# Another table of places: more sums by adding transfers, evictions on VectorE, loads on GpSimd's queue

## The chip, the cores and the metric

The kernel runs on one core of one Trainium2 chip. The metric is the device time of one execution in microseconds, and the figure used is the median over several runs. The core's engines are named as the profile names them: PE (TensorE, matrix products), PEld (its weight loads), DVE (VectorE), ACT (ScalarE), POOL (GpSimd) and SP (SyncE, which here only issues transfers). Each engine carries out its own instructions strictly in order; where one needs the result of another engine or of a transfer, it waits on a semaphore, and everything behind it on that engine waits too.

## What is computed

There are 2048 rows of 640 columns. The first half of the reference is a long convolution, done there by FFT, between a layer norm and a gate; the second half is a SwiGLU feed-forward network with a layer norm ahead of it. Both have a residual.

```python
def _A_ref(q, k, v, shift_k, ssm_k, ssm_D):        # B, S, D = 1, 2048, 640
    k_pad = jnp.pad(k, ((0, 0), (ks - 1, 0), (0, 0)))
    for t in range(ks):                            # ks = 4
        k_shift = k_shift + k_pad[:, t:t + S, :] * shift_k[:, ks - 1 - t][None, None, :]
    kv = k_shift * v
    ...
    y_f = kv_f * kf_f[None, :, :, :]
    y = irfft2(y_f, ...)[:, 0, :S, :]              # causal convolution of kv with ssm_k
    y = y + kv * ssm_D[None, None, :]
    return q * y

def _B_ref(x, w_gate, w_up, w_down):               # 640 -> 1728 -> 640
    g = _silu(x @ w_gate)
    u = x @ w_up
    return (g * u) @ w_down

x = A_q
h = x + _A_ref(_layernorm(x, axis=-1), A_k, A_v, A_shift_k, A_ssm_k, A_ssm_D)
h2 = h + _B_ref(_layernorm(h, axis=-1), B_w_gate, B_w_up, B_w_down)
return h2
```

## The kernel before

**Blocks.** The rows are cut into four blocks of 512 (0 to 3). A block lies in SBUF as 128 partitions with four rows each, a tile of 128x2560 elements in bf16 (640 KB). The convolution is done block by block in a transformed space of length 1024: the filter's block j gives the spectrum G_j, the input's block j the spectrum X_j, and block j of the output needs the products of all pairs X_i, G_(j-i).

**Stages of one block.** Block j runs through these steps; the lines are those of the profile.
- Loads of the filter (L289), k (L477 for block 0, transposing transfers for the others), v (L296) and q (L301). The filter is copied by rows on ACT and transposed by four transfers (L404); block 0's is transposed on PE (L411, evicted at L413).
- kv: four shifted products of k with a diagonal matrix on PE (L490, L492), evicted and multiplied by v.
- Spectra: matrix products with the table WF on PE (L329), each evicted from PSUM in the function `taken`, by ACT (L319) or by DVE (L322); then differences and sums of the halves on DVE (L361, L379, L386, L390, L393). L393 is the sum that may be a transfer.
- Products: for each pair, L539 or L542 on DVE multiplies two spectra (128x2560 for L542), and the sums of such products are L545. Two closing lines, L581 and L582, put real and imaginary parts together. Block 1 has two pairs, block 2 three, block 3 four.
- Inverse: L662, L663, L674 and L677 on DVE, matrix products with the table WI on PE (L698), a scaling on ACT (L707), and L709 on DVE, which multiplies by the normalised q, adds q and gives h.
- The second layer norm: sums of squares on ACT (L606), three small DVE steps (L644, L646, L648) with one on POOL between them (L610); the normalised row is written by ACT (L722) or DVE (L724), and transposed.
- Feed-forward of the block before, spread between the stages of the present one: gate and up products on PE (L769); Silu on ACT (L783); then either a copy of the up half on ACT (L785) with a product of two SBUF tiles on DVE (L787), or a product straight from PSUM on DVE (L786); L811 closes the last, half-wide chunk; the products with w_down on PE (L833, L845), the eviction on ACT (L850) and an adding store on GpSimd's queue (L852), or L862 and a plain store (L866) for the last block. Ahead of a block's adding stores, h itself is stored (L754).

**What sets the order.** The program first builds 923 operations in a `Plan`, each with its reads and writes, and then emits them in the order of the table `ORDER` (L48 to L90). The compiler leaves that order alone, so the table alone decides what stands behind what on each engine. An entry `i` emits operation i as built. An entry that is negative emits operation `~i` (that is -i-1) in its *other* form, which three kinds of operations and two single ones have:
- `evict` and `taken`, the row at L722 and the up half at L785 are built for ACT and have a form for DVE (for L785 that form is L786, and L787 falls away);
- `added` (sums L393 and L545 and the like) is built for DVE and has a form in which GpSimd's queue carries a transfer from one SBUF tile into another that adds on arrival (L243);
- `load` (L250) is built for SP's queue and has a form on GpSimd's.

```python
def added(ns, fn, to, what, reads, write, n=1):
    plan.add("dve", ns, fn, reads, [write], ("add", 2 * P * R * D * n,
        lambda: nc.gpsimd.dma_start(out=to(), in_=what(), accum_op=ALU.add, max_dma_last_dim=4 * D)))

def load(nbytes, fn, w, r=()):
    return plan.add("sp", nbytes, lambda: fn(nc.sync), r, w, ("pq", nbytes, lambda: fn(nc.gpsimd)))
```

**Places and queues.** Tiles of 640 KB come from an arena of 22 units; besides there are four PSUM slots of two banks, five row tiles and three tiles for the gate. A unit goes to the next user in the order of the table, and the user waits until the former one is done. SP's queue and GpSimd's have eight semaphores each (DMAHW0 to 7, DMASW0 to 7), used in turn: a transfer that would take a semaphore whose last transfer is still under way waits for it, and so do those behind it in the same queue. POOL also does a few small steps of its own (L610, L624, L634 to L636).

## Time and profile before

| | before |
|---|---|
| runs, us | 251.36, 251.21, 253.07 |
| median, us | 251.36 |
| span of the profiled execution, us | 251.4 |
| PE busy, us (share) | 237.3 (94%) |
| DVE busy | 197.7 (79%) |
| ACT busy | 173.9 (69%) |
| POOL busy | 54.0 (21%) |
| adding transfers between SBUF tiles (L243) | 11 |
| moved by SP's queue / GpSimd's, MB | 21.38 / 11.96 |

A busy share is an average over the whole span. Which engine sets the time is seen stage by stage: the stretch in which an engine has no idle time, and who waits for it there. The chain of waits that ended last goes back from the last instruction to what released it at each step, and so shows at which engine the path changes hands. A tile's buffer number is left out in the views (arena, ps, sg), so a line and an operation say what stands there.

### The profile page before, as it was taken

The page shows a single profiled execution, that of the slowest core. Times are in us where ns is not written, and L with a number is a line of the kernel's source. Part 1 is how long each engine was busy: PE and PEld are TensorE (multiplying, and loading weights), DVE is VectorE, ACT ScalarE, POOL GpSimd, SP SyncE. Part 2 cuts the span into 40 slices and gives each one's busy share as a digit, 9 for nine tenths or more (in the row PEclk, how much of TensorE's full clock was granted, in tenths as well). Part 3 has the DMA queues.
Part 4 walks back from the last instruction along what each step waited for, and adds up shares of the span by engine and source line. Part 5 has one row for each costly group of instructions (what it writes and reads, how often), then busy time and mean ns, then how long its engine had stood idle before and what let it go on. Part 6 is the DMA issues. An engine that isn't in the chain of part 4 may idle for free.

```text
span 251.4 us, 5138 instructions
## 1 busy us (share of the span) xinstructions
PE 237.3 (94%) x2113; PEld 153.0 (61%) x2125; DVE 197.7 (79%) x249; ACT 173.9 (69%) x300; POOL 54.0 (21%) x54
## 2 busy tenths in 40 slices
PE   3869997999999999999999999999999999999994
PEld 3447675788777677444465676454456785465662
DVE  2379999999999999999999989999999542131222
ACT  2449998999999976975988789983542865325100
POOL 0002003231540313220270404263612110000030
PEclk9999999999999999999999999999999999999999
DMA  5995699774998654685345468889592200000052
GB/s 156 376 212 163 127 324 352 231 197 92 165 246 292 202 81 81 105 154 133 79 66 146 86 99 194 148 146 163 98 224 29 26 0 3 0 0 3 0 78 78
DMA packets 37283, 33.66 MB, mean 134 GB/s; under 512 B 22470, under 2 KB 32076, under 8 KB 37260
## 3 DMA queue, kind: packets, MB, share of 16 engines
q1 hardware_dynamic: 31884, 21.38, 32.1%
q0 software_dynamic: 5376, 11.96, 25.9%
q8 instruction: 16, 0.26, 0.4%
q14 instruction: 7, 0.06, 0.1%
HBM read 16.29 MB, written 4.59 MB: 83 GB/s over the span
## 4 chain that ended last, share of the span: by engine, by line
PE 56%; ACT 17%; DMA 10%; DVE 9%; issue 4%; SPq 3%; DVEq 0%; ACTq 0%; POOLq 0%
PE ps L769 24%; PE ps L845 22%; ACT arena L319 7%; DMA arena<-in_A_ssm_k_dram 7%; PE ps L698 5%; DMA arena<-arena 3%; ACT sg L785 2%; PE ps L490 2%; SPq L404 2%; ACT junk L606 1%; PE ps L329 1%; PE ps L833 1%; DVE arena L674 1%; DVE arena L663 1%; DVE arena L662 1%
## 5 line engine op out<-in xcount | busy, mean ns | idle before, releaser
L769 PE MATMUL ps<-arena,wgu 128*128 128x512 bf16 (+1 forms) x668 | 116.7, 328 | 1.4 <-ACT sg L809 0.5
L769 PEld LDWEIGHTS <-wgu 128*128 128x128 bf16 x680 | 66.2, 98 | 45.3 <-issue 1.4
L845 PE MATMUL ps<-wd,tT 128*128 128x320 bf16 x416 | 59.1, 299 | 0.0
L845 PEld LDWEIGHTS <-tT 128*128 128x128 bf16 x416 | 39.8, 98 | 17.2 <-issue 1.8
L542 DVE TENSOR_TENSOR arena<-arena 128x2560 bf16<-128x2560 bf16 x30 | 44.1, 1484 | 0.2
L783 ACT ACTIVATE sg<-ps 128x1024 bf16<-128x1024 f32 (+1 forms) x28 | 26.9, 968 | 20.3 <-PE ps L769 19.7
L329 PE MATMUL ps<-arena,WF 128*128 128x320 bf16 x176 | 29.8, 299 | 1.2 <-ACT arena L319 0.9
L785 ACT CAST sg<-ps 128x1024 bf16<-128x1024 f32 (+1 forms) x23 | 23.0, 998 | 6.9 <-PE ps L769 3.1
L319 ACT CAST arena<-ps 128x320 bf16<-128x320 f32 (+1 forms) x48 | 25.2, 583 | 1.9 <-DVE arena L545 1.1
L610 POOL TENSOR_TENSOR sm<-sm,neghalf 128x4 f32<-128x4 f32 (+1 forms) x10 | 16.6, 1659 | 43.4 <-DVE sm L646 43.1
L787 DVE TENSOR_TENSOR tT<-sg,sg 128x1024 bf16<-128x1024 bf16 (+1 forms) x23 | 15.5, 673 | 11.5 <-ACT sg L785 11.5
L243 POOL DMA_DIRECT2D arena<-arena x11 | 13.3, 1211 | 47.4 <-DVE arena L542 11.2
L329 PEld LDWEIGHTS <-WF 128*128 128x128 bf16 x176 | 17.1, 98 | 10.0 <-issue 2.3
L606 ACT ACTIVATE junk<-arena 128x640 bf16<-128x640 bf16 x28 | 20.8, 744 | 1.3 <-DVE arena L709 1.3
L545 DVE TENSOR_TENSOR arena<-arena 128x2560 bf16<-128x2560 bf16 x14 | 20.7, 1487 | 0.2
L319 ACT ACTIVATE arena<-ps 128x640 bf16<-128x640 f32 (+1 forms) x32 | 20.2, 655 | 0.3
L698 PE MATMUL ps<-arena,WI 128*128 128x320 bf16 x96 | 15.7, 299 | 0.9 <-issue 0.6
L850 ACT ACTIVATE row<-ps,sm 128x640 bf16<-128x640 f32 x12 | 9.5, 791 | 8.2 <-PE ps L845 8.0
L709 DVE SCALAR_TENSOR_TENSOR arena<-arena,sm,ps 128x640 bf16<-128x640 bf16 x16 | 13.6, 876 | 1.8 <-ACT ps L707 1.8
L852 POOL DMA_DIRECT2D out_dram<-row x12 | 11.7, 1153 | 14.1 <-ACT row L850 14.1
L707 ACT ACTIVATE ps<-ps,sm 128x640 f32<-128x640 f32 x16 | 12.1, 770 | 3.7 <-PE ps L698 3.5
L698 PEld LDWEIGHTS <-WI 128*128 128x128 bf16 x96 | 9.0, 97 | 5.6 <-issue 1.3
(91 smaller groups left out, 240.8 us busy)
## 6 DMA issues: line engine op xcount, KB each, us to landing
arena<-arena POOLq DMA_DIRECT2D x11, 640.0 KB, 6.1
arena<-in_A_q_dram SPq DMA_DIRECT2D x4, 640.0 KB, 5.1
out_dram<-row POOLq DMA_DIRECT2D x13, 160.0 KB, 4.2
arena<-in_A_ssm_k_dram SPq DMA_DIRECT2D x3, 640.0 KB, 9.4
arena<-in_A_v_dram SPq DMA_DIRECT2D x3, 640.0 KB, 6.3
wd<-in_B_w_down_dram SPq DMA_DIRECT2D x2, 800.0 KB, 7.3
out_dram<-arena POOLq DMA_DIRECT2D x2, 640.0 KB, 5.8
wgu<-in_B_w_gate_dram SPq DMA_DIRECT2D x1, 800.0 KB, 6.5
```

The source lines that it names most:

```text
L319: (lambda: nc.scalar.activation(dst(), src(), ACT.Copy, scale=2.0)) if twice else (lambda: nc.scalar.copy(dst(), src())),
L329: nc.tensor.matmul(ap(ps)[:, h, 0:NH], w, ap(src)[:, r, h * NH:(h + 1) * NH], start=(first and i == 0), stop=(last and i == len(rs) - 1), ...
L542: dve(1402, lambda: v.tensor_mul(to(), X.part(xs), H.part(hs)), [X.at(xs), H.at(hs)], [at])
L545: added(1402 * n - 69 * (n - 1), lambda: v.tensor_add(to(), to(), b()), to, b, [what], at, n)
L606: act(725, lambda r=r: nc.scalar.activation(waste(), ap(x)[:, r, :], ACT.Square, scale=D ** -0.5, accum_out=sm(s, MSQ, (r,))), [(x, r)], [ ...
L610: nc.gpsimd.tensor_tensor(sm(s, RSTD, rs), sm(s, VAR, rs), ap(neghalf)[:, 0:len(rs)], op=ALU.pow)
L698: nc.tensor.matmul(ap(ps)[:, w, 0:NH], m, src[:, w * NH:(w + 1) * NH], start=(i == 0), stop=(i == len(terms) - 1))
L769: nc.tensor.matmul(split(ap(ps), n)[:, i, :], w(k), ap(hT)[:, k, lo:lo + n], start=(k == 0), stop=(k == KT - 1))
L783: act(905 if wide_ else 490, lambda: nc.scalar.activation(of(sg), of(*gate), ACT.Silu), [(gate[0], gate[1] + i) for i in range(m)] + (psu ...
L785: op = plan.add("act", 905 if wide_ else 490, lambda: nc.scalar.copy(of(co), of(*up)), psu + [sg], [co] + tt, ("dve", 1135 if wide_ else 6 ...
L787: op.rest = dve(602 if wide_ else 336, lambda: nc.vector.tensor_mul(to(), of(sg), of(co)), [sg, co], tt)
L845: nc.tensor.matmul(ap(ps[hf])[:, hf, 0:NH], ap(tT)[:, c * BLK + at:c * BLK + at + P], ap(wd)[:, c, hf * NH:(hf + 1) * NH], start=False, st ...
```

## The change

Only the table `ORDER` differs; no operation is added or taken away, and PE carries out the same products. It places most of the 923 operations in another order, and takes other forms:
- Adding transfers instead of DVE sums: 22 instead of 11. Block 1 has six (two before), block 2 seven (two), block 3 nine (seven).
- Twenty evictions more are DVE's than before (26 go from ACT to DVE, six go back). To DVE go two transposes of block 0 (L413), six half-wide L319s of block 0's spectra and six whole ones of later blocks (then L322), six rows of L722 (then L724), and six up halves of L785 (then L786 in the place of L785 and L787).
- GpSimd's queue carries 18 loads and plain stores instead of five. Sixteen are new on it: the taps, block 0's filter, the skip weights, block 0's q and one half of WI at the start; four loads of FFN weights; q of blocks 1 to 3; block 2's filter; and three stores of output rows of the last block. Three go back to SP's: block 0's store of h, and block 3's filter and v.

The first rows of the table, of 43 that all change:

```diff
-    0, 1, 2, 3, 16, 18, -20, 5, 4, 8, 17, 186, 9, 20, 22, 7, 10, 11, -22, 24, -26, 23, 26, 75, 76, 13, 15, 12, 6,
-    77, 78, 79, 193, 80, 81, 82, 34, 35, 14, 38, -40, 36, -38, 92, 32, 27, 93, 96, 97, 40, -42, 88, 89, 30, 94,
...
+    -9, 16, 5, 0, 3, 9, 10, 18, 19, -16, 7, 11, 20, 17, 24, 25, -13, -22, 1, 22, -24, 26, 75, 2, 76, 77, 6, 78, 79,
+    80, 83, 81, 186, 82, 36, 34, 40, 13, 37, -36, -42, 109, 42, 14, 88, 96, 38, -40, 110, 111, -113, 32, 89, 90,
...
```

SP's queue at the start, before: k's two halves (L477), the taps (L889), block 0's filter (L289), v (L296), the tables WF (L903) and WI (L909), the skip weights (L904), block 1's filter (the second L289) and q (L301).

```order
L477 DMA arena_86<-in_A_k_dram 128x1280
L889 DMA arena_86<-in_A_shift_k_dram 5x512
L477 DMA arena_86<-in_A_k_dram 128x1280
L289 DMA arena_86<-in_A_ssm_k_dram 128x5x512
L296 DMA arena_86<-in_A_v_dram 128x2560
L903 DMA WF_88<-const_wf 128x1024
L904 DMA arena_86<-in_A_ssm_D_dram 1x640
L289 DMA arena_86<-in_A_ssm_k_dram 128x5x512
L903 DMA WF_88<-const_wf 128x1024 [waits DMAHW0_49]
L301 DMA arena_86<-in_A_q_dram 128x2560 [waits DMAHW1_49]
L909 DMA WI_89<-const_wi 128x1024 [waits DMAHW2_49]
L909 DMA WI_89<-const_wi 128x1024 [waits DMAHW3_49]
```

The same queue after, down to the first load that waits for a semaphore. L404 is a transposing transfer of block 1's k, L737 a load of FFN weights.

```order
L477 DMA arena_86<-in_A_k_dram 128x1280 x2
L296 DMA arena_86<-in_A_v_dram 128x2560
L289 DMA arena_86<-in_A_ssm_k_dram 128x5x512
L903 DMA WF_88<-const_wf 128x1024 x2
L404 DMA_TRANSPOSE kT_93<-in_A_k_dram 128x5x128 [waits Activation_49]
L909 DMA WI_89<-const_wi 128x1024
L737 DMA wgu_95<-in_B_w_up_dram 128x5x512 [waits DMAHW0_49]
```

And GpSimd's queue after, from its first transfer to the load of block 2's filter (the second L289); before, this engine had no transfer ahead of its 13th row, block 0's store of h. L872, L875, L624 and L610 are POOL's own steps.

```order
L889 DMA arena_86<-in_A_shift_k_dram 5x512
L872 ISA
L872 AFFINE_SELECT ident_87<-ident_87 128x128 [waits DVE_49]
L904 DMA arena_86<-in_A_ssm_D_dram 1x16x40
L289 DMA arena_86<-in_A_ssm_k_dram 128x5x512
L301 DMA arena_86<-in_A_q_dram 128x2560
L909 DMA WI_89<-const_wi 128x1024
L875 MEMSET neghalf_99 128x4
L624 TENSOR_SCALAR sm0_76<-sm0_76 128x4 [waits DVE_49]
L610 TENSOR_TENSOR sm0_76<-sm0_76,neghalf_99 128x4 [waits Pool_49]
L289 DMA arena_86<-in_A_ssm_k_dram 128x5x512 [waits DMAHW1_49,DMAHW0_49,PE_49]
```

The taps, the skip weights, block 0's filter, q and one half of WI have moved from SP's queue to GpSimd's; behind k, SP's now has v, block 1's filter and WF.

DVE in block 1's products, before: from the last L542 behind a gate product (L787) to the start of the inverse (L662). A wait on DMASW is one on a transfer of GpSimd's queue, one on DMAHW of SP's.

```order
L542 TENSOR_TENSOR arena_86<-arena_86 128x2560
L787 TENSOR_TENSOR tT_94<-sg0_69,sg1_70 128x4x256 [waits Activation_49]
L545 TENSOR_TENSOR arena_86<-arena_86 128x2x1280 [waits DVE_49] x2
L787 TENSOR_TENSOR tT_94<-sg2_71,sg0_69 128x4x256 [waits Activation_49]
L581 TENSOR_TENSOR arena_86<-arena_86 128x2x1280 [waits DVE_49]
L542 TENSOR_TENSOR arena_86<-arena_86 128x2560 [waits DMASW0_49]
L811 TENSOR_TENSOR tT_94<-sg0_69,sg2_71 128x256 [waits Activation_49]
L582 TENSOR_TENSOR arena_86<-arena_86 128x2x1280 [waits DMASW2_49,DVE_49]
L787 TENSOR_TENSOR tT_94<-sg1_70,sg0_69 128x4x256 [waits Activation_49]
L662 TENSOR_TENSOR arena_86<-arena_86 128x2560 [waits DVE_49]
L663 TENSOR_TENSOR arena_86<-arena_86 128x2560 [waits DVE_49]
```

DVE at the same place after, from an L542 behind the pair product L539 down to L662; L379 and L386 are differences within a spectrum of the next block's transform.

```order
L542 TENSOR_TENSOR arena_86<-arena_86 128x2560 [waits DMASW2_49]
L542 TENSOR_TENSOR arena_86<-arena_86 128x2560 [waits DMASW3_49]
L787 TENSOR_TENSOR tT_94<-sg1_70,sg0_69 128x4x256 [waits Activation_49]
L542 TENSOR_TENSOR arena_86<-arena_86 128x2560 [waits PE_49]
L811 TENSOR_TENSOR tT_94<-sg2_71,sg1_70 128x256 [waits Activation_49]
L379 TENSOR_TENSOR arena_86<-arena_86 128x640 [waits DMASW5_49]
L386 TENSOR_TENSOR arena_86<-arena_86 128x2x640 [waits Activation_49]
L542 TENSOR_TENSOR arena_86<-arena_86 128x2560 [waits DMASW4_49,DVE_49]
L581 TENSOR_TENSOR arena_86<-arena_86 128x2x1280 [waits DMASW5_49]
L787 TENSOR_TENSOR tT_94<-sg0_69,sg2_71 128x4x256 [waits Activation_49]
L582 TENSOR_TENSOR arena_86<-arena_86 128x2x1280 [waits DMASW7_49,DVE_49]
L662 TENSOR_TENSOR arena_86<-arena_86 128x2560 [waits DVE_49]
```

The sums (L545) are gone from this stretch, and six rows wait on DMASW, for transfers of GpSimd's queue: two L542, L379, a third L542, L581 and L582.

GpSimd's queue in block 1, before, between block 0's store of h (L754) and block 1's second layer norm (L634 to L610).

```order
L754 DMA out_0_dram<-arena_86 128x2560 [waits DMAHW1_49]
L243 DMA arena_86<-arena_86 128x2x1280 [waits DMAHW2_49,DMAHW0_49,DMAHW7_49,DVE_49,PE_49]
L243 DMA arena_86<-arena_86 128x2x1280 [waits DMASW1_49,DVE_49,Activation_49]
L634 TENSOR_TENSOR sm1_77<-sm1_77 128x4 [waits Activation_49]
L635 TENSOR_TENSOR sm1_77<-sm1_77 128x4 [waits Activation_49,Pool_49]
L636 TENSOR_SCALAR sm1_77<-sm1_77 128x4 [waits Pool_49]
L610 TENSOR_TENSOR sm1_77<-sm1_77,neghalf_99 128x4 [waits Pool_49]
```

The same place after: L737, L746 and L749 are loads of FFN weights, L301 that of block 1's q.

```order
L737 DMA wgu_95<-in_B_w_gate_dram 128x5x576
L243 DMA arena_86<-arena_86 128x2x1280 [waits DVE_49,Activation_49]
L610 TENSOR_TENSOR sm1_77<-sm1_77,neghalf_99 128x2 [waits DVE_49]
L737 DMA wgu_95<-in_B_w_up_dram 128x5x576 [waits DMASW0_49]
L301 DMA arena_86<-in_A_q_dram 128x2560 [waits DMAHW4_49,DMAHW2_49,DMAHW5_49,DMASW1_49,DMAHW6_49,PE_49,Activation_49]
L610 TENSOR_TENSOR sm2_78<-sm2_78,neghalf_99 128x2 [waits DVE_49]
L243 DMA arena_86<-arena_86 128x2x1280 [waits DMASW2_49,DVE_49,Activation_49]
L243 DMA arena_86<-arena_86 128x2x1280 [waits DMASW3_49,DVE_49]
L243 DMA arena_86<-arena_86 128x2x1280 [waits DMASW4_49,DVE_49]
L243 DMA arena_86<-arena_86 128x2x1280 [waits DMASW5_49,DVE_49]
L749 DMA wd_97<-in_B_w_down_dram 64x640 [waits DMASW6_49]
L243 DMA arena_86<-arena_86 128x2x1280 [waits DMAHW4_49,DMAHW2_49,DMAHW5_49,DMASW7_49,DMAHW7_49,DMASW3_49,DVE_49]
```

Six adding transfers (L243) now stand in this queue where two stood, with loads of weights between them, and block 0's store of h has left it.

80 rows, old and new, of the table ORDER are left out of this document.

## The prediction

> **What bounds the kernel now.** I read the page's busy shares first, then the busy time of each engine by stage, then the chain of work that ended last, and last the transfers. The profiled execution spans 251.4 us against a median of 251.36 us over the runs, so nothing lies around the span and the sum below starts from 251.4. A measurement of this kernel can tell about 1% from no change.
>
> Busy time by stage; the columns are PE, its weight loads, DVE, ACT, POOL, clock, DMA share, GB/s:
>
> ```profile
> 0.00:15.00 15.00, 7.93 (x174) 5.25 (x175) 5.80 (x16) 4.68 (x4) 0.54 (x6) 1.00 0.94 281
> 15.00:45.00 30.00, 28.15 (x342) 19.64 (x343) 28.67 (x54) 27.76 (x65) 3.92 (x3) 1.00 0.85 229
> 45.00:70.00 25.00, 24.29 (x221) 20.92 (x220) 24.57 (x23) 24.91 (x44) 8.96 (x5) 1.00 0.71 161
> 70.00:100.00 30.00, 29.85 (x354) 21.33 (x353) 28.87 (x36) 26.09 (x46) 6.50 (x8) 1.00 0.69 183
> 100.00:136.00 36.00, 35.50 (x182) 17.77 (x186) 35.27 (x34) 30.02 (x47) 9.91 (x9) 1.00 0.56 103
> 136.00:185.00 49.00, 48.79 (x412) 27.44 (x415) 47.65 (x48) 36.69 (x64) 18.62 (x18) 1.00 0.76 142
> 185.00:251.40 66.40, 62.79 (x438) 40.70 (x440) 26.86 (x43) 23.76 (x35) 5.51 (x7) 1.00 0.17 36
> ```
>
> PE is the bound at the granted clock 1.00, but it is not alone. In the first 15 us it waits for loads; from 45 to 70 ACT has 0.09 us of idle time in 25; from 45 to 136 DVE has 0.43 + 1.13 + 0.73 = 2.3 us of idle time in 91. Whatever holds DVE up there soon holds PE up. The chain shows where:
>
> ```profile
> 3.90 11.01 DMA arena<-in_A_ssm_k_dram
> ...
> 63.21 1.03 ACT sg L785
> ...
> 71.23 1.41 DVE arena L662
> 72.67 1.49 DVE arena L663
> ...
> 77.83 1.61 DVE arena L709 x4
> 79.48 2.34 PE ps L769 x20
> ...
> 129.03 1.50 DVE arena L662
> 130.56 1.50 DVE arena L663
> ...
> 135.11 0.81 DVE arena L709 x2
> 135.96 0.45 PE ps L833 x4
> ```
>
> The chain starts with a load, runs through ACT up to 70 us, and twice passes through DVE at L662 to L709: that is where blocks 1 and 2 end their products and PE's inverse (L698) starts. After 136 us it is PE's own work. So the time is settled at two places, block 1's inverse and block 2's: how much work and waiting DVE has ahead of them, less what PE has ahead.
>
> **The change, part by part.** *The start.* Before, all first loads stand in SP's queue, block 0's filter fourth, WF's halves sixth and ninth.
>
> ```profile
> 2.52 0.52 SPq L296 DMA_DIRECT2D arena<-in_A_v_dram  x1
> 4.33 2.19 SPq L903 DMA_DIRECT2D WF<-const_wf  x1
> 11.13 3.15 DVE L513 TENSOR_TENSOR arena<-ps,arena 128x512 bf16<-128x512 f32 x6 [3.83 <-DMA arena<-in_A_v_dram]
> 14.96 1.03 PE L411 MATMUL ps<-ident,arena 128*128 128x128 bf16 x15 [2.98 <-DMA arena<-in_A_ssm_k_dram]
> 15.82 0.82 PE L329 MATMUL ps<-arena,WF 128*128 128x320 bf16 x4
> ```
>
> Now block 0's filter goes out on GpSimd's queue with q and half of WI behind it, and on SP's v, block 1's filter and WF follow k. PE's first L329 then waits for WF. By the 281 GB/s of the first stage, 2.5 MB of SP's and some 1.2 MB of GpSimd's are 13 to 14 us, against 15.82 now: a gain of about 1.9 us. The ends are 0 (all of both queues' bytes first) and 4.5 us (SP's own bytes alone, 2.5 MB after a first landing at 2.5 us). I take 1.9.
>
> *ScalarE's work.* Twenty evictions leave ACT.
>
> ```profile
> L319 ACT CAST arena<-ps 128x640 bf16<-128x640 f32 x24 | 16.3, 711 | 1.9 <-DVE arena L545 1.1 <-PE ps L329 0.7
> L722 ACT ACTIVATE row<-arena,sm 128x640 bf16<-128x640 bf16 x10 | 8.9, 928 | 2.5 <-DVE sm L648 2.5
> L724 DVE TENSOR_SCALAR row<-arena,sm 128x640 bf16<-128x640 bf16 x6 | 2.5, 444 | 0.1
> L786 DVE TENSOR_TENSOR tT<-sg,ps 128x1024 bf16<-128x1024 bf16 x2 | 2.4, 1222 | 6.2 <-PE ps L769 6.2
> L787 DVE TENSOR_TENSOR tT<-sg,sg 128x1024 bf16<-128x1024 bf16 x22 | 15.1, 685 | 11.5 <-ACT sg L785 11.5
> L513 DVE TENSOR_TENSOR arena<-ps,arena 128x512 bf16<-128x512 f32 x4 | 2.5, 683 | 3.8 <-DMA arena<-in_A_v_dram 3.8
> ```
>
> A 128x640 eviction from PSUM on DVE is not in this trace; L413's 0.49 us for bf16 and L513's 0.683 x 640/512 = 0.85 us bound it, and I take 0.8, the f32 row. A normalised row is 0.44 us on DVE for 0.93 on ACT; a gate product straight from PSUM is 1.22 for 0.685 plus an ACT copy. Along the built order that takes about 13 us from ACT and gives DVE about 10.5. It frees the stretch from 45 to 70 us, but the chain leaves ACT at 70 us, so it is worth nothing by itself if DVE is late at 71.
>
> *DVE's sums.* Eleven additions less are 11 x 1.48 = 16 us of DVE.
>
> ```profile
> L542 DVE TENSOR_TENSOR arena<-arena 128x2560 bf16<-128x2560 bf16 x30 | 44.1, 1484 | 0.2
> L243 POOL DMA_DIRECT2D arena<-arena x11 | 13.3, 1211 | 47.4 <-DVE arena L542 11.2 <-DVE arena L545 10.7 <-ACT wodd L741 9.6
> arena<-arena POOLq DMA_DIRECT2D x11, 640.0 KB, 6.1
> 105.09 0.34 issue
> 105.43 5.67 DMA arena<-arena
> DVE arena L662 <- DMA arena<-arena: 0.3, 1, 0.3
> ```
>
> With evictions in and sums out, I added the durations of the rows along both built orders. Ahead of block 1's last L709 DVE had 1.2 us more work than PE, now 0.5 more; ahead of block 2's first L698 it had 0.6 less, now 1.2 less. That is a gain of 0.7 us at either place, no more: PE's rows were moved up as well.
>
> *The new waits.* This is the term that decides. An adding transfer takes 0.3 us and more to be issued after its producer and 5.67 (that one) to 6.1 us (the median) to land: 6.0 at least, 6.3 to 6.9 as a rule. Before, DVE had over 7 us of other work between producer and user in blocks 1 and 2, and waited 0.3 us in all. Now, in block 1, the product of the first L542 is used after one L542, two L724s, L539 and L787, 5.5 us from start to start, and the next three after 4.8 us each (L542 or L582 behind L542, L787, L811, L379, L386). DVE is in order, so a wait moves what follows. With 6.5 us a transfer, and 2.7 us between two landings of this queue, the five waits add to 3.7 us (1.8 with 6.0 us and no queue, 5.5 with 7.2). G2's own sum adds 0.4 (0.1 to 1). Block 2's five (4.9, 5.9, 5.9, 8.2 and 5.4 us of cover) add 3.1 (1.8 to 4.5). Together 7.2 us, between 3.7 and 11. Block 3's nine wait too, some 5 us, but there DVE has 7 us and more in hand on PE, so they cost nothing. About half of the 2.3 us that DVE idles now between 45 and 136 us goes under in these waits: 1.2 (0 to 1.7).
>
> A rule to weigh here. The row says 6.1 us for 640 KB. The Trainium skill (DMA: Bandwidth & Descriptors, section on the anatomy of one DMA, SWDGE path) fits such a transfer as about 2.0 us plus its bytes over 436 GB/s; an estimate by that page is 3.5 us, all waits in blocks 1 and 2 would be covered, and the sum would come to the time of the first rival below. The trace does not agree with it for adding transfers, and the row is used.
>
> *Queues.* GpSimd's queue gets 24 more issues, some 1.2 us each, 29 us in all; POOL is idle for most of the span, so they cost only where two stand together, which is in the waits above. SP's queue gets shorter. *The tail* keeps its last store on SP: 0.
>
> The sum: -1.9 - 0.7 + 7.2 - 1.2 = +3.4 us, **254.8 us**.
>
> **The rivals.** *The transfers hide (faster).* If landing takes less than about 5 us, the waits shrink to 1 us in all and the sum is -1.9 - 0.7 + 1.0 - 1.2 = -2.8, 248.6 us. It decides from the point where a transfer fits in the 4.8 us of cover. Against it: the quickest row is 5.67 us after issue. Chance 0.18.
>
> *The start gives more.* If WF lands with SP's bytes alone, the start is 4.5 us shorter and the sum is -4.5 - 0.7 + 7.2 - 1.2 = +0.8, 252.2 us, no change. For it: two queues share the transfer engines from 2 us on; against it: the engines already move 281 GB/s over these 15 us. Here also lies the case that the waits are near 4 us. Chance 0.26.
>
> *GpSimd's queue falls behind.* Its own instructions stretch under a busy DVE:
>
> ```profile
> 66.10 3.97 POOL L634 TENSOR_TENSOR sm<-sm 128x4 f32<-128x4 f32 x1 [2.77 <-ACT junk L629]
> 162.78 1.02 POOL L634 TENSOR_TENSOR sm<-sm 128x4 f32<-128x4 f32 x1
> ```
>
> If the transfers do so too, each of the three spaced waits in block 1 and in block 2 grows by 0.8 us and more, +5 in all: 259.8 us. The one sign against it: L243's 1.21 us was measured with DVE nearly full. Chance 0.14. The Trainium skill (SBUF — State Buffer, section on the two separate sides) says that a DVE operation in a two-port mode locks GpSimd out while it writes descriptors, so that a transfer of 0.62 us took 3.1; by it these waits would grow by some 2.5 us each. POOL's L634 agrees with the direction, the issues of L243 do not.
>
> **How the numbers follow.** My own case has 0.42, with its own range of 253 to 258; 0.07 of it lies within 1% (under 253.9). So slower by over 1%: 0.35 + 0.14 = 0.49; within 1%: 0.26 + 0.07 = 0.33; faster by over 1% (under 248.85): 0.18. All low ends together give -4.5 - 0.7 + 3.7 - 1.7 = -3.2, 248.2; all high ends 0 - 0.7 + 11 - 0 = +10.3, 261.7. They won't all meet: 248.5 to 259.3 leaves out 0.2, half of it the lower part of the first rival.
>
> **What would show it.** Right: the first L329 at 13 to 15 us; DVE waits on adding transfers at L542, L581 and L582 of block 1 (3 to 5 us) and at L542 and L581 of block 2 (2 to 4 us); PE idle just before block 1's and block 2's L698 and L833; ACT with idle time from 45 us on. Wrong: issue to landing under 5 us; DVE idle under 3 us between 45 and 136 us; or PE waiting for ACT or for weights of the FFN, which I have at nothing because the loads of wgu land on both queues well ahead of the L769s that use them.

## The result, and the profile after

| | before | after |
|---|---|---|
| runs, us | 251.36, 251.21, 253.07, 251.35 | 282.62, 280.11, 284.45, 282.56 |
| median, us | 251.36 | 282.59 |
| ratio, with its 95% interval | 1 | 1.120 (1.114 to 1.126) |
| span of the profiled execution, us | 251.4 | 280.6 |
| mean granted clock of PE | 1.000 | 0.978 |

The kernel became slower by 31 us, where 3.4 were forecast and 8 stood at the upper end of the range. In each pair of a run and its own profile that can be put side by side the run is about 2 us longer than the span (282.62 against 280.6), so the remark in the prediction that nothing lies around the span was wrong. By this, before's profiled execution of 251.4 us was its longest run, 253.07, and a difference of spans against it comes out some 2 us short (29.2 for 31). Below, spans are compared with spans and medians with medians. Runs over 1.5% above the fastest of their kernel, one of after's four among them, are left out of the ratios and of the medians below (after's is then 282.56), while the texts of what was expected quote medians of all runs.

First the busy shares on the page of after, then its stretches as the prediction showed them for before (columns: PE, weight loads, DVE, ACT, POOL, clock, DMA share, GB/s):

```profile
PE 244.8 (87%) x2114; PEld 155.2 (55%) x2125; DVE 194.5 (69%) x253; ACT 163.6 (58%) x281; POOL 71.5 (25%) x78
```

```profile
0.00:15.00 15.00, 8.98 (x189) 6.29 (x190) 5.73 (x16) 4.94 (x7) 3.84 (x11) 1.00 0.76 271
15.00:45.00 30.00, 26.42 (x312) 17.73 (x311) 26.75 (x52) 26.95 (x55) 7.17 (x7) 1.00 0.88 192
45.00:70.00 25.00, 19.63 (x172) 15.74 (x171) 17.36 (x22) 19.18 (x35) 5.45 (x6) 1.00 1.09 298
70.00:100.00 30.00, 24.23 (x173) 18.05 (x174) 23.75 (x29) 17.77 (x32) 9.17 (x12) 0.89 0.80 168
100.00:136.00 36.00, 31.40 (x313) 18.31 (x314) 28.50 (x30) 21.85 (x40) 12.14 (x11) 0.95 0.81 147
136.00:185.00 49.00, 45.37 (x405) 26.51 (x406) 41.25 (x43) 33.86 (x56) 11.81 (x12) 1.00 0.68 129
```

Three things are to be read here. PE and DVE both have idle time in every stretch, where before DVE had 2.3 us of it between 45 and 136 us; now it has 21.4. The transfer engines' share between 45 and 70 us rose from 0.71 to 1.09, the highest of the run. And the granted clock falls below 1.00 in two stretches. PE's share of the loss: the span grew by 29.2 us, of which 21.7 are idle time of PE (280.6 − 244.8 against 251.4 − 237.3) and 7.5 are more busy time for the same products.

The chain of waits names the place (columns: start, length, what):

```profile
57.51 14.56 DMA arena<-arena
72.09 1.49 DVE arena L542
73.58 0.60 DVE tT L787
74.19 1.40 DVE arena L542
75.88 8.41 DMA arena<-arena
84.39 1.50 DVE arena L582
85.91 1.49 DVE arena L662
...
134.11 6.90 DMA arena<-arena
141.03 1.50 DVE arena L581
```

Ahead of block 1's first L662 stand two adding transfers of 14.56 and 8.41 us. DVE's timeline at this place (start, length, row, and in brackets its idle time and what ended it):

```profile
67.25 1.49 DVE L542 TENSOR_TENSOR arena<-arena 128x2560 bf16<-128x2560 bf16 x1 [4.50 <-DMA arena<-arena]
72.09 1.49 DVE L542 TENSOR_TENSOR arena<-arena 128x2560 bf16<-128x2560 bf16 x1 [3.35 <-DMA arena<-arena]
73.50 0.68 DVE L787 TENSOR_TENSOR tT<-sg,sg 128x1024 bf16<-128x1024 bf16 x1
```

DVE comes to block 1's first L662 at 85.9 us instead of 71.2. Its busy time up to there is the same in both kernels, 59.7 us; its idle time went from 11.5 to 26.2. Of that, waits on adding transfers are 12.2 (0 before), waits for PE 10.1 (5.3), for ACT 2.5 (1.1), for loads 0 (3.9). Up to block 2's first L662 (144.1 against 129.0 us) the adding transfers' waits come to 15.6, so block 2's own are 3.4.

From DVE the wait runs on to PE through the gate. The product L787 stands behind the waiting L542; it frees a tile sg; ACT's L810 writes that tile, and PE's L769 needs ACT to have read its PSUM slot. The two rows from the timelines of ACT and of PE, and then the same moments in stretches of 2 us (columns as above):

```profile
74.22 0.74 ACT L810 CAST sg<-ps 64x256 bf16<-64x256 f32 x2 [6.65 <-DVE tT L787]
75.02 4.21 PE L769 MATMUL ps<-arena,wgu 128*128 128x256 bf16 x19 [6.32 <-ACT sg L810]
```

```profile
70.00:72.00 2.00, 0.00 (x0) 0.00 (x0) 0.00 (x0) 0.00 (x0) 0.23 (x1) 1.00 1.31 123
72.00:74.00 2.00, 0.00 (x0) 0.00 (x0) 1.91 (x2) 0.00 (x0) 0.12 (x1) 0.97 1.11 211
74.00:76.00 2.00, 0.98 (x5) 0.71 (x5) 2.00 (x4) 1.74 (x4) 1.78 (x3) 0.50 0.66 122
76.00:78.00 2.00, 2.00 (x12) 1.41 (x10) 2.00 (x3) 2.00 (x6) 2.00 (x2) 0.50 1.08 191
78.00:80.00 2.00, 2.00 (x11) 1.45 (x10) 0.33 (x1) 2.00 (x5) 0.03 (x1) 0.50 1.07 192
80.00:82.00 2.00, 2.00 (x17) 1.64 (x16) 1.95 (x2) 1.10 (x4) 0.73 (x2) 0.83 1.14 201
```

For 2 us no compute engine but POOL works at all, and when PE starts again its clock is 0.50 for 6.83 us. What else lay on the transfer engines stands in the list of transfers issued from 53 to 70 us (count, size of one, median us to landing):

```profile
arena<-arena POOLq DMA_DIRECT2D x3, 640.0 KB, 10.9
wd<-in_B_w_down_dram SPq DMA_DIRECT2D x1, 800.0 KB, 16.3
arena<-in_A_q_dram POOLq DMA_DIRECT2D x1, 640.0 KB, 7.2
out_dram<-arena SPq DMA_DIRECT2D x1, 640.0 KB, 8.0
wd<-in_B_w_down_dram SPq DMA_DIRECT2D x1, 80.0 KB, 7.1
kT<-in_A_k_dram SPq DMA_TRANSPOSE x2, 11.6
```

An adding transfer alone takes about 6 us; in this crowd three took 10.9 in the median, one of them 14.56.

### The profile page after: what moved, and what is told of

Same layout as the page of the kernel before. It is cut to its first block, busy times and chain, and to the rows that moved or that the text cites. A ratio compares the mean times of both kernels' runs of the same rounds, so it can differ in the third digit from the quotient of the medians.

```text
span 280.6 us, 5145 instructions
## 1 busy us (share of the span) xinstructions
PE 244.8 (87%) x2114; PEld 155.2 (55%) x2125; DVE 194.5 (69%) x253; ACT 163.6 (58%) x281; POOL 71.5 (25%) x78
## 4 chain that ended last, share of the span: by engine, by line
PE 36%; DMA 26%; DVE 20%; issue 6%; SPq 4%; ACT 3%; POOL 2%; POOLq 0%; ACTq 0%; DVEq 0%
DMA arena<-arena 18%; PE ps L769 14%; PE ps L845 13%; PE ps L329 5%; DVE arena L542 5%; DMA WF<-const_wf 5%; SPq L404 3%; PE ps L698 3%; DMA arena<-row 2%; DVE arena L582 2%; DVE arena L662 2%; DVE tT L787 2%; POOL arena L243 2%; DVE arena L545 2%; PE ps L490 1%
## 5 line engine op out<-in xcount | busy, mean ns | idle before, releaser
L769 PE MATMUL ps<-arena,wgu 128*128 128x256 bf16 (+1 forms) x669 | 118.5, 334 | 12.7 <-ACT sg L810 6.3
L769 PEld LDWEIGHTS <-wgu 128*128 128x128 bf16 x680 | 67.7, 100 | 59.5 <-issue 13.8
L845 PE MATMUL ps<-wd,tT 128*128 128x320 bf16 x416 | 61.2, 303 | 1.4 <-DVE tT L787 1.1
L542 DVE TENSOR_TENSOR arena<-arena 128x2560 bf16<-128x2560 bf16 x30 | 44.3, 1487 | 12.5 <-DMA arena<-arena 12.3
L243 POOL DMA_DIRECT2D arena<-arena x22 | 26.7, 1254 | 91.1 <-DVE arena L542 38.5
L329 PE MATMUL ps<-arena,WF 128*128 128x320 bf16 x176 | 29.6, 299 | 5.5 <-DMA arena<-arena 2.3
L785 ACT CAST sg<-ps 128x1024 bf16<-128x1024 f32 (+1 forms) x18 | 17.8, 989 | 14.4 <-DVE tT L787 10.8
L329 PEld LDWEIGHTS <-WF 128*128 128x128 bf16 x176 | 16.9, 97 | 14.2 <-issue 3.9
L319 ACT CAST arena<-ps 128x640 bf16<-128x640 f32 (+1 forms) x43 | 23.0, 582 | 1.9 <-PE ps L329 1.8
L787 DVE TENSOR_TENSOR tT<-sg,sg 128x1024 bf16<-128x1024 bf16 (+1 forms) x18 | 12.1, 672 | 13.8 <-ACT sg L785 13.8
L319 ACT ACTIVATE arena<-ps 128x640 bf16<-128x640 f32 (+1 forms) x25 | 16.0, 652 | 6.6 <-PE ps L329 6.4
L610 POOL TENSOR_TENSOR sm<-sm,neghalf 128x4 f32<-128x4 f32 (+1 forms) x10 | 14.5, 1451 | 18.0 <-DVE sm L646 17.6
L698 PE MATMUL ps<-arena,WI 128*128 128x320 bf16 x96 | 15.5, 299 | 1.0 <-DVE arena L674 1.0
L852 POOL DMA_DIRECT2D out_dram<-row x12 | 12.7, 1181 | 12.5 <-ACT row L850 12.5
L786 DVE TENSOR_TENSOR tT<-sg,ps 128x1024 bf16<-128x1024 bf16 (+1 forms) x10 | 10.6, 1057 | 6.3 <-PE ps L769 5.0
L698 PEld LDWEIGHTS <-WI 128*128 128x128 bf16 x96 | 9.2, 98 | 5.9 <-DVE arena L674 1.6
```

What stands on the lines that cost most here:

```text
L319: (lambda: nc.scalar.activation(dst(), src(), ACT.Copy, scale=2.0)) if twice else (lambda: nc.scalar.copy(dst(), src())),
L329: nc.tensor.matmul(ap(ps)[:, h, 0:NH], w, ap(src)[:, r, h * NH:(h + 1) * NH], start=(first and i == 0), stop=(last and i == len(rs) - 1), ...
L542: dve(1402, lambda: v.tensor_mul(to(), X.part(xs), H.part(hs)), [X.at(xs), H.at(hs)], [at])
L610: nc.gpsimd.tensor_tensor(sm(s, RSTD, rs), sm(s, VAR, rs), ap(neghalf)[:, 0:len(rs)], op=ALU.pow)
L698: nc.tensor.matmul(ap(ps)[:, w, 0:NH], m, src[:, w * NH:(w + 1) * NH], start=(i == 0), stop=(i == len(terms) - 1))
L769: nc.tensor.matmul(split(ap(ps), n)[:, i, :], w(k), ap(hT)[:, k, lo:lo + n], start=(k == 0), stop=(k == KT - 1))
```

## The experiments

Each kernel is after with one edit, unless it says before. Numbers in the table `ORDER` name operations, and a number's sign its form, as told above. The ratio is to before in the same session, with its 95% interval.

| run | edit | median, us | ratio |
|---|---|---|---|
| e1_order_only | after's order, all forms of before | 304.44 | 1.210 (1.199 to 1.221) |
| e2_forms_only | before's order, after's forms | 332.47 | 1.318 (1.310 to 1.326) |
| e3_adds_as_before | the 11 adding transfers of before | 292.24 | 1.159 (1.150 to 1.168) |
| e7_evictions_as_before | the evictions' forms of before | 295.03 | 1.172 (1.168 to 1.176) |
| e9_loads_as_before | the loads' queues of before | 281.89 | 1.118 (1.113 to 1.124) |
| e6_start | WF ahead of block 1's filter, taps on SP's queue | 283.74 | 1.124 (1.118 to 1.131) |
| e12_before_start | before, its start's loads on GpSimd's queue | 252.46 | 1.004 (1.000 to 1.007) |
| e4_block1_sums | block 1's four new transfers as sums | 274.34 | 1.086 (1.078 to 1.094) |
| e8_blocks12_sums | and block 2's four among products | 276.55 | 1.097 (1.091 to 1.102) |
| e10_218_sum | of block 1's four the filter's sum alone | 281.03 | 1.114 (1.108 to 1.121) |
| e11_products_sums | of block 1's four the three product sums | 281.75 | 1.117 (1.111 to 1.124) |
| e5_uncrowded | a store and a load out of the crowd | 279.76 | 1.112 (1.107 to 1.118) |
| e13_block1_left_out | block 1's four left out | 275.36 | 1.098 (1.090 to 1.107) |
| e14_blocks12_left_out | and block 2's six | 268.02 | 1.062 (1.056 to 1.069) |
| e15_new_left_out | and block 3's five | 267.32 | 1.060 (1.053 to 1.067) |
| e16_plain_copies | every adding transfer a plain copy | 262.77 | 1.043 (1.034 to 1.051) |
| e17_left_out_uncrowded | e14, with e5's move | 263.98 | 1.050 (1.046 to 1.055) |
| e18_254_258_too | e14, and block 1's two old transfers left out | 261.71 | 1.038 (1.030 to 1.046) |

No version is faster than before.

### Which part of the change

The first three take the table apart: its order with the old forms, the old order with its forms, and the sums alone. One line of each; e2's is a line of before's table:

```diff
-    80, 83, 81, 186, 82, 36, 34, 40, 13, 37, -36, -42, 109, 42, 14, 88, 96, 38, -40, 110, 111, -113, 32, 89, 90,
+    80, 83, 81, 186, 82, 36, 34, 40, 13, -38, 35, -42, 109, 42, 14, 88, 96, 38, -40, 110, 111, 112, 32, 89, 90,
...
```

```diff
-    251, 337, 170, 176, 312, 333, 340, 341, 185, 416, 259, 323, 327, 171, 261, 172, 256, 326, 322, 329, 330, 269,
+    -252, 337, -171, 176, 312, 333, 340, 341, 185, 416, 259, 323, 327, 171, 261, 172, 256, 326, 322, 329, 330, 269,
...
```

```diff
-    131, 132, 138, 216, 206, 211, 217, 416, 418, 143, 412, -219, 180, 144, 137, 141, 142, 139, 224, 229, 146, 417,
+    131, 132, 138, 216, 206, 211, 217, 416, 418, 143, 412, 218, 180, 144, 137, 141, 142, 139, 224, 229, 146, 417,
...
```

> The changed order with every form of before (11 adding transfers, loads and evictions where they were). If the forms make the loss (the waits for adding transfers and what crowds them), most of it is gone: 251 to 260 us. If the order makes it (transfers standing at bad places whatever their queue), it stays over 270 us.

> The order of before with every form of the change (22 adding transfers, 18 loads on GpSimd's queue, 20 more evictions on DVE). If the forms make the loss, 268 to 290 us; if the order makes it, 250 to 260 us.

> The change with the adding transfers of before alone (11 instead of 22); loads and evictions as changed. DVE gets 16 us of sums back. If the new adding transfers make the loss, some 20 us of waits go and up to 12 us of DVE work comes onto the path: 262 to 274 us. If it is the loads' queues or the order, over 277 us.

All three are worse than after, by 10 to 50 us, and e2 lies above both ranges that were named. Two groups of DVE's waits point to why, the second largest of e1 and then the largest of e2 (columns: us in total, times, longest):

```profile
DVE arena L361 <- ACT arena L319: 14.3, 2, 9.8
```

```profile
DVE arena L542 <- DMA arena<-arena: 21.4, 7, 5.1
```

In e1 evictions that went back to ACT stand just ahead of DVE's users; in e2 transfers stand just ahead of theirs. Order and forms fit only each other, so such halves cannot be added up to the change, and e3 is no clean test either: four sums that are no transfers in after become transfers right ahead of their users. What can be said by them is small: neither half alone explains 31 us. The later runs therefore keep the order and change few forms.

Then the evictions alone (e7) and the loads alone (e9), one line of each:

```diff
-    -92, 97, 193, 98, 101, -103, -28, 43, -100, -45, 51, 52, 103, 104, 30, -29, 59, 60, 45, 187, 46, 53, 54, 113,
+    91, 97, 193, 98, 101, 102, -28, 43, 99, 44, 51, 52, 103, 104, 30, -29, 59, 60, 45, 187, 46, 53, 54, 113,
...
```

```diff
-    -9, 16, 5, 0, 3, 9, 10, 18, 19, -16, 7, 11, 20, 17, 24, 25, -13, -22, 1, 22, -24, 26, 75, 2, 76, 77, 6, 78, 79,
+    8, 16, 5, 0, 3, 9, 10, 18, 19, 15, 7, 11, 20, 17, 24, 25, 12, -22, 1, 22, -24, 26, 75, 2, 76, 77, 6, 78, 79,
...
```

> The change with the evictions where they were before: ACT gets 13 us back, DVE gives 10.5 us. If DVE's work is on the path between its waits, 274 to 279 us; if ACT becomes the bound, or what DVE saves goes into the same waits, 282 us or more.

> The change with every load and plain store on the queue it had before (five on GpSimd's instead of 18). If the loads in GpSimd's queue delay the adding transfers, those of block 1 land within 9 us and the time falls to 272 to 279 us. If the order was fitted to the two queues, SP's queue now holds up the transposing transfers behind waiting loads, and the time rises to 285 us or more.

e7 is 12 us slower than after: DVE's waits for ACT up to block 3's first L662 are 41.5 us against 9.0. Its largest group of waits over the whole span is this one:

```profile
DVE tT L787 <- ACT sg L785: 22.6, 8, 5.9
```

So the evictions on DVE are not the loss; this order needs them. e9 does not differ from after within the intervals. It shows one thing on GpSimd's queue: an adding transfer, ready at 127.34 us, was issued 5.4 us late, because a load of block 3's filter stood ahead of it there and waited for PE (POOL's timeline):

```profile
131.85 0.94 POOL L289 DMA_DIRECT2D arena<-in_A_ssm_k_dram  x1 [5.74 <-PE ps L769]
132.78 1.27 POOL L243 DMA_DIRECT2D arena<-arena  x1
```

In after no adding transfer waited like that in blocks 1 and 2: each was issued within 0.6 us of the last thing that it needed, or right behind the one before it in the queue.

### The start

e6 puts WF ahead of block 1's filter on SP's queue; e12 gives before the loads that the change sends by GpSimd's queue.

```diff
-    80, 83, 81, 186, 82, 36, 34, 40, 13, 37, -36, -42, 109, 42, 14, 88, 96, 38, -40, 110, 111, -113, 32, 89, 90,
+    80, 83, 81, 13, 14, 186, 82, 36, 34, 40, 37, -36, -42, 109, 42, 88, 96, 38, -40, 110, 111, -113, 32, 89, 90,
...
```

```diff
-    0, 1, 2, 3, 16, 18, -20, 5, 4, 8, 17, 186, 9, 20, 22, 7, 10, 11, -22, 24, -26, 23, 26, 75, 76, 13, 15, 12, 6,
+    0, 1, 2, 3, 16, 18, -20, 5, 4, -9, 17, 186, 9, 20, 22, 7, 10, 11, -22, 24, -26, 23, 26, 75, 76, 13, -16, -13, 6,
...
```

> The change with WF ahead of block 1's filter in SP's queue and the taps back on SP's queue. WF has 640 KB less ahead of it: the first L329 some 2 us earlier (14.5 to 15.5 us instead of 16.8). If the start is passed on to the end, 279.5 to 281 us; if the waits for adding transfers in block 1 take it up, no change (282 to 283 us).

> The kernel before with five first loads alone (taps, block 0's filter, skip weights, q, half of WI) on GpSimd's queue, as in the change. If two queues bring the first tables earlier, the first L329 stands at 13 to 15 us and the time is 249 to 250.5 us. If the transfer engines are full in these 15 us anyway, 251 to 252.5 us. If descriptors written by GpSimd come later, 253 us or more.

Neither gains. In after PE's first L329 come at 14.93 us, but the run of them at 16.82, behind a wait of 1.46 for WF, against 15.82 before. Kernels whose opening is the same as after's have this second row at 14.0 us (e4), 15.64 (e16), 16.82 (after) and 17.98 (e15): a scatter of 4 us, more than the gain in question. e6 has the row at 15.78, inside that scatter, so its one trace does not show whether block 1's filter ahead of WF holds it. e12's trace is of an execution of 356.5 us at a granted clock of 0.65 and says nothing of its start.

### Block 1's and block 2's waits

The four new sums of block 1 are the filter's (218) and three of products (251, 260, 262). e4 makes all four DVE's again, e10 and e11 the one or the three, e8 adds four of block 2 (482, 484, 489, 491). Two of e4's lines:

```diff
-    430, 431, 239, 424, 183, 250, -252, 338, 253, -255, 337, 269, 322, 411, 432, 433, 334, 160, -168, -171, 255,
+    430, 431, 239, 424, 183, 250, 251, 338, 253, -255, 337, 269, 322, 411, 432, 433, 334, 160, -168, -171, 255,
...
-    -263, 267, 263, -185, 361, 314, 362, 363, 348, 344, 265, 316, 266, 185, 315, -259, -183, 264, 274, 342, 268,
+    262, 267, 263, -185, 361, 314, 362, 363, 348, 344, 265, 316, 266, 185, 315, -259, -183, 264, 274, 342, 268,
```

> The change with four of block 1's six adding transfers done as sums on DVE again (5.9 us of DVE work). If these transfers' own waits cost the 9 to 14 us by which PE falls behind there, 272 to 277 us, and DVE's idle time from 60 to 85 us goes from 12 to under 4 us. If the engines are full anyway, so that the two that are left are as late, 279 us or more.

> The change with eight adding transfers of blocks 1 and 2 as sums on DVE again (11.8 us of DVE work). If the waits cost more than the sums in block 2 as in block 1, 266 to 272 us, under the 274.4 us of the kernel with block 1's four alone. If DVE is the bound in block 2 by then, 274 to 284 us.

> The change with one adding transfer, that of block 1's filter spectrum at 40 us, as a sum on DVE again (1.5 us). If it crowds out the transposing transfers of block 2's filter, those issued from 38 to 46 us land in 3 to 5.5 us instead of 6 to 8, PE's wait at about 49 us goes, and the time is 278.5 to 281 us. If it has no share, 282 to 284 us.

> The change with three of block 1's adding transfers, those of its products at 56, 69 and 74 us, as sums on DVE again (4.4 us). If the waits for them and for the one between them cost most of the 8 us that the four together gave back, 275 to 278 us, and no L542 of block 1 waits over 4 us. If they cost only what the sums cost, 281 us or more.

e4 gains 8 us: DVE does 4.8 us more work up to block 1's first L662 (64.5 us) and comes there at 77.1 instead of 85.9, with 12.5 us of idle time. Of the adding transfers one wait is left there:

```profile
64.33 1.49 DVE L542 TENSOR_TENSOR arena<-arena 128x2560 bf16<-128x2560 bf16 x1 [3.36 <-DMA arena<-arena]
```

Either part alone gains 1 to 1.5 us, which the intervals do not tell from nothing; both together 8. So there are two late points of about equal length side by side; which they are is read off the traces, not shown by a run. One is the filter's sum: its transfer, under way from 39.9 to 47.8 us, meets the four transposing transfers of the filter on SP's queue. Those issued from 37 to 46 us, of after and then of e10:

```profile
arena<-arena SPq DMA_TRANSPOSE x3, 7.0
```

```profile
arena<-arena SPq DMA_TRANSPOSE x4, 4.7
```

The other is the chain through L542 that was shown above. Taking one away leaves the other. In e10, two product transfers still took 13.1 and 15.2 us. e8 is not faster than e4: block 2's four sums cost DVE as much as the waits that they end.

### The crowd at 53 to 70 us

e5 sends block 0's store of h by GpSimd's queue and moves the load of w_down (181) to that queue, behind block 1's last transfer.

```diff
-    -263, 267, 263, -185, 361, 314, 362, 363, 348, 344, 265, 316, 266, 185, 315, -259, -183, 264, 274, 342, 268,
+    -263, 267, 263, -185, 361, 314, 362, 363, 348, 344, 265, 316, 266, 185, 315, -259, -182, -183, 264, 274, 342, 268,
...
```

> The change with two of SP's transfers (block 0's store of h, 640 KB, and the first 800 KB of w_down) put on GpSimd's queue behind block 1's adding transfers, so that 1.4 MB fewer are under way from 55 to 72 us. If block 1's adding transfers are late because the transfer engines are full, the second of them lands within 10 us of its issue instead of 14.6, and the time falls to 275 to 279 us. If they are late because of their own queue or their own work, they land as late as before and the time stays over 280 us.

The three transfers that took 10.9 us in the median (after) now take, over the same window,

```profile
arena<-arena POOLq DMA_DIRECT2D x3, 640.0 KB, 7.1
```

so the crowd is shown to be what stretched them. DVE's longest wait at an L542 falls from 4.5 to 1.7 us. But the median falls by only 2.8 us, which the intervals hardly tell from nothing, and block 1's first L662 comes at 84.3: by the trace, the filter's late transposes, three of the four 6.8 to 7.8 us long here, are the late point that remains.

### Left out, and copied

To see what the waits and the engines' load cost with DVE's work unchanged, transfers were left out altogether, in three steps, and in e16 each adds nothing (a plain copy of the same bytes on the same queue). The edits of e13 and of e16; e14's tuple goes on with 441, 442, 482, 484, 489 and 491, e15's with 683, 684, 688, 699 and 701:

```diff
-HTURN = (1, 2)
+HTURN = (1, 2); LEFT = (218, 251, 260, 262)
...
-            if op.fn:
+            if op.fn and op.n not in LEFT:
```

```diff
-        plan.add("dve", ns, fn, reads, [write], ("add", 2 * P * R * D * n, lambda: nc.gpsimd.dma_start(out=to(), in_=what(), accum_op=ALU.add, max_dma_last_dim=4 * D)))
+        plan.add("dve", ns, fn, reads, [write], ("add", 2 * P * R * D * n, lambda: nc.gpsimd.dma_start(out=to(), in_=what(), max_dma_last_dim=4 * D)))
```

> The change with block 1's four new adding transfers left out altogether: nothing is added in their place, so DVE has no more work and GpSimd's queue and the transfer engines have 2.5 MB less. If block 1's transfers cost what PE falls behind there, about 11 to 13 us go: 269 to 272 us. If DVE's sums in the kernel with these four as sums cost nothing, it is no better than that kernel's 274.4 us.

> The change with block 1's four and block 2's six new adding transfers left out. If block 2's cost as much as PE falls behind there (9 us from 100 to 150 us), 259 to 264 us. If PE falls behind there by the order itself, 267 us or more.

> The change with all fifteen adding transfers left out that the kernel before does not have. This is what the change would take if they were hidden. If they are the whole loss, 248 to 254 us; if the order and the other forms have a share, 256 us or more, and that share is what is left over 251.4 us.

> The change with each adding transfer as a plain copy of the same tile (nothing is added). If the adding on arrival makes a transfer long, a copy lands 3 to 4.5 us after its issue where nothing else is under way, and the time falls to 265 to 275 us. If it is the bytes and the crowding, it lands in 5.5 us or more as before, and the time is over 279 us.

By medians block 1's four cost 7.2 us, block 2's six 7.3, block 3's five 0.7, which is within the scatter. e13 lies within 1.0 us of e4, so block 1's four sums on DVE are nearly free, and as transfers they cost all that leaving them out gains. With all fifteen left out, e15 still takes 15 us more than before by its ratio: about half of the loss is not in the new transfers. In e16, whose trace is of its longest run (269.88 us), the page's transfers and DVE's largest group of waits on them:

```profile
arena<-arena POOLq DMA_DIRECT2D x22, 640.0 KB, 4.1
```

```profile
DVE arena L542 <- DMA arena<-arena: 0.5, 2, 0.2
```

Copies land in 3.4 to 4.4 us in the open, adding transfers in 5.7 to 6.3. With 0.5 us of waits in all, some 20 of the 31 us are gone, and 11 are left. Even copies took 9.8 and 10.4 us in the crowd of block 1.

With e14's ten left out, one old transfer of block 1 still holds DVE for 5.89 us in front of an L542. e17 therefore adds e5's move to e14, and e18 leaves out block 1's two old transfers (254, 258) as well.

> The change with the ten new adding transfers of blocks 1 and 2 left out, and with two of SP's transfers (block 0's store of h and the first 800 KB of w_down) behind block 1's adding transfers on GpSimd's queue. If the crowding from 50 to 70 us is what is left, the old adding transfer of block 1's first sum lands within 8.5 us of its issue instead of 11.4, DVE's wait for it falls from 8 to 5 us or less, and the time from 268.5 to 262 to 266 us. If the crowding has no share, 267 us or more.

> The change with the ten new adding transfers of blocks 1 and 2 left out, and block 1's two old ones too, so that block 1 has none. If the wait for the first of them is what holds DVE and PE at 55 to 75 us, 259 to 264 us, and PE is behind by 16 us or less of its own work where block 1's inverse starts (20 with them). If PE's lag is made before (the start, the filter's transposes, ScalarE), 266 us or more.

They gain 4.0 and 6.3 us on e14 by the medians, e18's being that of two runs 3.3 us apart. In e17 the wait shrinks, and the page's row of the granted clock has no break left:

```profile
61.49 1.49 DVE L542 TENSOR_TENSOR arena<-arena 128x2560 bf16<-128x2560 bf16 x1 [0.71 <-DMA arena<-arena]
```

```profile
PEclk9999999999999999999999999999999999999999
```

The kernels with after's order can be laid side by side, since PE has the same rows in the same order. The start of the first L698 of each block's inverse in PE's timeline, and the span:

| | block 1 | block 2 | block 3 | span |
|---|---|---|---|---|
| after | 90.86 | 151.66 | 220.54 | 280.6 |
| e4 | 82.01 | 143.80 | 210.75 | 270.6 |
| e13 | 82.73 | 145.09 | 212.62 | 272.5 |
| e14 | 83.25 | 136.09 | 204.66 | 264.6 |
| e15 | 87.16 | 140.03 | 207.77 | 267.3 |
| e17 | 78.72 | 131.56 | 200.11 | 260.2 |
| before (other order) | 75.55 | 132.97 | 194.44 | 251.4 |

Each edit gains at its own block and keeps nearly all of it to the end: 8.1 us from after to e13 at block 1, 9.0 from e13 to e14 at block 2, 4.5 from e14 to e17 at block 1. Behind block 3's first L698 all six have 59.5 to 60.1 us left (before 57.0). So a loss ahead of block 1's or block 2's inverse is a loss at the end. But e15, which up to block 2 is the same kernel as e14, comes to block 1's inverse 3.9 us later, behind a start with 6.83 us at half clock from 16.0 us on. So 4 us between two single traces can be scatter, and e17's gain rests on the ratios, 1.062 and 1.050, whose intervals do not meet.

e17 still stands 8.8 us over before by the spans, though it does less adding and has no break in the clock. Followed along PE's work, some 5 us of that are four steps of 0.9 to 2.0 us of idle time spread over the span, and 2.9 are more busy time of PE. The last 1.1 lie behind PE's last product, where e17 takes 4.6 us (after 4.5) and before 3.5. There e9, whose stores have before's queues, takes 3.5 again, so this part is the queue of the last stores. The rest was not undone by any run and stays open.

## Why the prediction was wrong

Two steps failed. The term of the new waits, 7.2 us, was sized by landing times from an uncrowded kernel, and the ten new transfers of blocks 1 and 2 cost 14 us. And the rest of the change, its order with the other forms, was put at a gain of 2.6 us (1.9 at the start and 0.7), and without any new transfer it takes 15 us more than before.

- **The time at which a transfer lands: wrong, and the largest part that is shown.** "An adding transfer takes 0.3 us and more to be issued after its producer and 5.67 (that one) to 6.1 us (the median) to land." The first half held (0.6 us and less). The second took the price from a kernel in which a transfer met little else. In block 1 the transfers took 10.85, 14.56, 6.41, 6.14 and 8.41 us, because their own number, two loads of weights, q, a store and two transposing transfers of k lay on the same engines; e5 shows that with two of these gone the median of three is 7.1. DVE's waits in block 1 were 12.2 us for 4.1 forecast. Only spacing in GpSimd's queue was priced ("2.7 us between two landings of this queue"), not the other queue's transfers, and no row shows the 2.7: in after, adding transfers issued within 1.7 us of each other landed 3.3 to 4.9 us apart.
- **Block 2's waits: right in size, wrong in effect.** 3.4 us for 3.1. But leaving block 2's six out gains 7.3 by the medians. In e13, which still has them, DVE waits 5.4 us there for adding transfers, and a gap of 3.9 us on PE is followed by 6.83 us at half clock; in e14 it is 0.7 us, and no such piece.
- **The way to PE: missed.** The sum let a wait of DVE reach PE at the inverse alone. It reached it earlier, through L787, a tile sg and ACT's L810 to L769. The prediction named this as what would make it wrong, "PE waiting for ACT or for weights of the FFN, which I have at nothing", and looked only at when the weights land.
- **The order and the other forms: put at a gain of 0.7 us behind the start.** That figure came from adding up the durations of the rows along both orders, so waits that the order makes had no place in it. e15 takes 15 us more than before without any new transfer, and e16 11 us more with 0.5 us of DVE's waits on transfers. Some 4 of the 15 us are the crowd around block 1's old transfer (e17), and 1 us is the tail; what the rest is was not shown.
- **The clock: no term at all.** Behind gaps of 6.3 and 1.7 us PE's clock stood at 0.50 for 6.83 and 3.41 us, 10.24 us in all, which is 5.1 us of work lost, most of PE's 7.5 us of additional busy time.
- **The start: −1.9, measured +1.0.** The first L329 came at 14.93 us, inside the 13 to 15 named, but the row behind it waited for WF till 16.82. e4, with the same opening, has it at 14.0, so the term is smaller than its scatter. The argument also had block 0's and block 1's filter the wrong way round, in the prediction and in the part on the change: in before's queue the fourth transfer is block 1's filter, and block 0's is the eighth, issued at 3.90 us and landed at 14.91.
- **Idle time of DVE that takes up the waits: −1.2, not seen.** DVE's idle time from 45 to 136 us grew by 19 us, more than its waits on transfers.
- **DVE's own work: right.** 59.7 us up to block 1's first L662 in both kernels, where 0.7 us of gain had been worked out against PE's work, and an eviction of 128x640 took DVE 0.82 us for the 0.8 taken. ACT did get idle time from 45 us on, 5.8 us up to 70.
- **Block 3: about right.** Its five new transfers cost 0.7 us or nothing (e15), where nothing was forecast.
- **The tail: 0, measured +1.0.** Its last store is on SP's queue, as said, but three stores ahead of it went to GpSimd's queue, and from PE's last product to the end after takes 4.5 us, before and e9 3.5.
- **The rivals.** That GpSimd's queue falls behind: no, its L243 are 1254 ns against 1211, and none in blocks 1 and 2 stood long behind another. The rule of the Trainium skill weighed there (SBUF — State Buffer, section on the two separate sides) is not tested: no view tells in which mode a DVE operation ran, and the issues hardly stretch. That the transfers hide: even with e16's waits of 0.5 us the kernel takes 263 us, not the 248.6 of that rival, so its sum, too, lacked what the rest of the change costs by itself. And the estimate of 3.5 us for 640 KB, from the fit in the Trainium skill (DMA: Bandwidth & Descriptors, section on the anatomy of one DMA), which the prediction set aside, fits e16's plain copies in the open (3.4 to 4.4 us) and no adding transfer.

What is shown: by e13 and e14, that the ten new transfers of blocks 1 and 2 cost 14 us; by e17, some 4 more from the crowd of loads around block 1; by e5, that the crowd stretches the transfers; by e9, 1 us at the tail. What is only argued: how the 14 us divide between DVE's waits, the filter's transposes and the half clock. Some 9 to 13 us of the 31 (by e17's span, by its median) have no shown cause but for that 1 us.

## What to carry over

A transfer that takes over work of a full engine has to be priced at the load that the transfer engines have at its place, with all queues counted: where their share was already 0.71, four more in one block, with loads moved beside them, made it 1.09 and some of the transfers twice as long. When an in-order engine gets a new wait, list everything behind that wait that frees a buffer for another engine; the way through a small tile can be shorter than the way that the change was about. And test a table of places a few entries at a time, since halves of it can each be slower than the whole.

## What the runs showed of the hardware

- The granted clock is 1.00 or 0.50 in these traces, the latter in pieces of 3.41 us or a multiple of it; the one exception is e12's profiled execution, at 0.65 for 345 us, whose cause stays open. In after a gap of 6.3 us on PE was followed by 6.83 us at 0.50 and one of 1.7 us by 3.41; in e8 a gap of 2.2 us by 3.41, in e3 one of 9.7 by 10.24, in e2 one of 11.1 by 13.65. A gap of 2.8 us in after and one of 3.0 at the start of before were followed by none, so the length of a gap does not decide alone. Before and e17 have no such piece up to PE's last product. The Trainium skill (TensorE: Matmul & The Clock Gate, section on what's actually happening) describes a free-running window of 3413 ns behind which an idle PE gets half its pulses; these pieces agree. Where the Trainium skill (TensorE: Matmul & The Clock Gate, section on why this matters for your kernels) puts the harmful gap at over some 3 us, 1.7 us were enough in after.
- A transfer that adds costs about 2.2 us more than a copy of the same 640 KB on the same queue (medians 6.3 us in several of these kernels, 4.1 in e16). In block 1's crowd, two adding transfers of after took 10.9 and 14.6 us, at an engines' share of 1.09 from 45 to 70 us, and two copies of e16 took 9.8 and 10.4, at 0.97.
